# First MoE's blocks in written order on ACT, DVE, POOL and SP, and the second MoE's weight preparation in nine stages

## The chip, the cores and the metric

One core of a Trainium2 chip. TensorE (PE) multiplies, VectorE (DVE), ScalarE (ACT) and GpSimd (POOL) do the elementwise work, SyncE (SP) issues the DMA transfers. The metric is the device time of one execution in microseconds; lower is better.

## What is computed

Chunked local attention over 3072 tokens (4 x 768, 8 heads of 64), whose output runs through two feed-forward layers one behind the other.

```python
for c in range(nc):                       # chunks of 32 queries
    k_full = concat([mem_k, k[c_start-16 : c_end+8]]); v_full = ...
    a = softmax(scale * q_c @ k_full.T)
    out[c] = a @ v_full
x = out.transpose(0, 2, 1, 3).reshape(3072, 512)
h = x @ w_in                              # first MoE, 512 -> 2048 -> 512
x = relu(h) ** 2 @ w_out
g = x @ w_gate                            # second MoE, 512 -> 1536 -> 512
return (g * sigmoid(g) * (x @ w_val)) @ w_out2
```

## The kernel before

Tokens are cut into 8 blocks of 384. The first MoE's hidden dimension has 16 parts f of 128. A step is one (block t, part f): PE does the twelve hidden matmuls of the step two ahead (`hidden_pe`, L389) and then the twelve output matmuls of this one (`project_pe`, L433). Every product is three float32r passes over a high and a low half, so each operand is split into two. After the hidden matmuls ACT reads their PSUM bank (`hbank`, two of them, by parity of f) with relu (L397), squares it twice (L403 into the high half `gh`, L408), and DVE subtracts to get the low half `gl` (L414). PE's hidden matmuls two steps on write the same bank.

A step has four quarters: at each of four points between PE's half products the function `side(hs)` writes the side work of quarter `hs`. A block has 64 quarters. Side work is of two kinds:

- Attention for the next block, four units a block, 16 quarters apart. One quarter (e, the 1st, 17th, 33rd, 49th) has the value matmuls of one unit (`at_pv`, L286) and the scores of the next (`at_scores`, L164, both into `abank`); then come at e+1 the two halves of the result (x_hi on ACT L297, x_lo on DVE L301), e+2 the maximum (DVE L231, L232), e+3 and e+5 four exponentials each (ACT L240), e+7 the normalisation (DVE L253, L254, L258), e+8 and e+10 seven transposes (DVE L267), e+16 the next value matmuls. Query and key loads (`at_load`, L139) and value loads (`at_load_v`, L145) stand at e+8 for the unit due at e+16 (on SP). At the ends of a sequence DVE also sets a border of the scores (L170, L173).
- The second MoE's weights, 18 chunks of 1 MB, four to a block from block 2 on. `load2` loads a chunk (L104) 11 quarters ahead of its quarter a (4, 18, 32, 44 in a block); `prep2` at a then makes from 64-bit words float32 (`convert`: ACT scales L114, DVE shifts L115 and joins L117), four sums (POOL L478) and splits (ACT copies L481 `head`, L483 `cut`, L486 `wraw`, each with a POOL subtraction L482, L484, L487), and stores them to DRAM (`w2d`, L491, 6 to 8 transfers). Loads and block results share two `raw` buffers.

PE's instructions are in written order throughout. For the opening (a written token list) and the second MoE all engines are in written order too. In between, from step 14 of block 0 to the end of the first MoE, ACT, DVE, POOL and SP are ordered by the framework's scheduler, by its own priorities and costs: it may place an operation of `prep2` ahead of or behind relus, exponentials and loads.

In the last block's quarters the input of the second MoE is loaded, summed and split (`load_z`, `split_b1`, `sum_t`, `split_t`) and its first weights are loaded (`load_chunks`). The second MoE itself (L586, L637) is not touched.

Of the kernel before, what the change touches and what calls it, by code (L numbers as in the profile page):

```python
# [7 lines left out]
F32 = mybir.dt.float32  # L8
I32 = mybir.dt.int32
U16 = mybir.dt.uint16  # L10
R = mybir.dt.float32r
AF = mybir.ActivationFunctionType
ALU = mybir.AluOpType
# [19 lines left out]
CB = 2  # L33
# [11 lines left out]
QC = 2 * 128  # L45
# [6 lines left out]
WC = 1024  # L52
# [16 lines left out]
def attention_moe_moe_kernel(ctx, tc, att, v0, w1, w2, out):  # L69
# [9 lines left out]
    pe, act, dve, pool, sp = nc.tensor, nc.scalar, nc.vector, nc.gpsimd, nc.sync  # L79
# [4 lines left out]
    rawp = ctx.enter_context(tc.tile_pool(name="rawp", bufs=RB))  # L84
    dp = ctx.enter_context(tc.tile_pool(name="dp", bufs=1, space=DRAM))
    ps = ctx.enter_context(tc.tile_pool(name="ps", bufs=1, space=PSUM))
    w2d = dp.tile([128, NCH, 2, QC], F32, name="w2d")
# [14 lines left out]
    def load_w(src):  # L102
        t = rawp.tile([128, RAW], I32, tag="raw", name="wraw")
        sp.dma_start(out=t, in_=src.bitcast(I32))  # L104
        return t

    def convert(raw):

        words = raw.rearrange("p (n w) -> p w n", w=2)
        lower, upper = words[:, 0], words[:, 1]
        x = upper.bitcast(F32)
        act.activation(x, x, AF.Prelu, scale=2.0 ** -112, alpha=-(2.0 ** 32))  # L114
        dve.tensor_scalar(lower, lower, 29, None, ALU.logical_shift_right)  # L115
        w = rawp.tile([128, WC], F32, tag="cut", name="cut", bufs=CB)
        dve.scalar_tensor_tensor(w.bitcast(I32), upper, 3, lower, ALU.logical_shift_left, ALU.bitwise_or)  # L117
        return w


    actx = ctx.enter_context(ExitStack())
    ap = actx.enter_context(tc.tile_pool(name="ap", bufs=1))
# [202 lines left out]
    for t, n in enumerate(BLOCKS[1:], 1):  # L325
        for j in range(n):
            e = 13 * j + 12 if t == 1 else QB * (t - 1) + (j + 1) * QB // n - 15
# [12 lines left out]
    w = {}  # L340
# [76 lines left out]
    def hidden(t, f, between):  # L417
        hidden_pe(t, f, range(6))
        between()
        hidden_pe(t, f, range(6, 3 * KD))  # L420
        for fn in (relu, square, square_again, square_lo):
            fn(t, f)
# [15 lines left out]
    def project(t, f, between):  # L438
        n = nt_of[t]
        project_pe(t, f, range(6))  # L440
        between()
        project_pe(t, f, range(6, 3 * KD))
        y = [ybank[e][:, 0:n] for e in range(KD)]
        if f == NF1 - 1:
            t0 = blk0[t] * GQ
            ys = rawp.tile([128, RAW], F32, tag="raw", name="ys")[:, 0:KD * n].rearrange("p (k n) -> p k n", k=KD)
            for k in range(0, KD, 2):
                act.copy(ys[:, k], y[k])
                dve.tensor_copy(ys[:, k + 1], y[k + 1])
            sp.dma_start(out=y1d[:, :, t0:t0 + n], in_=ys)  # L450
# [6 lines left out]
    def load2(c):  # L457
        w["raw2", c] = load_w(w2[c])

    def prep2(c):  # L460
        raw = w.pop(("raw2", c))
        a = convert(raw)
        b0, b1, b2, b3 = (a[:, i * QC:(i + 1) * QC] for i in range(4))
        sums = raw.bitcast(F32)[:, 0:4 * QC]
        o0, o1, o2, o3 = (sums[:, i * QC:(i + 1) * QC] for i in range(4))
        j, kind = divmod(c, 3)
        if kind < 2:
            jobs = ((o2, b3, b2, ALU.add), (o0, o2, b0, ALU.subtract), (o1, b0, b3, ALU.subtract), (o3, b1, o0, ALU.subtract))
            first = 7 * (2 * j + kind)
            places = [w2d[:, first:first + 3:2], w2d[:, first + 5:first + 6], w2d[:, first + 1:first + 4:2], w2d[:, first + 4:first + 7:2]]  # L470
            parts = ((0, 2), (2, 4))
        else:
            jobs = ((o3, b3, b0, ALU.subtract), (o0, b2, o3, ALU.subtract), (o1, b2, b3, ALU.subtract), (o2, o0, b1, ALU.subtract))
            wo = w2d[:, GVC:].rearrange("p (i n) h c -> p i n h c", n=NP)[:, :, j]
            places = [wo[:, 0:2], wo[:, 6:7], wo[:, 2:6]]
            parts = ((0, 4),)
        for o, x, y, op in jobs:
            pool.tensor_tensor(o, x, y, op)  # L478
        head = ap.tile([128, 2 * QC], R, tag="head", name="head")
        pieces = [(a[:, 0:2 * QC], head), (b2, b3.bitcast(R))]  # L480
        act.copy(head, a[:, 0:2 * QC])  # L481
        pool.tensor_tensor(a[:, 0:2 * QC], a[:, 0:2 * QC], head.bitcast(F32), ALU.subtract)  # L482
        act.copy(b3.bitcast(R), b2)  # L483
        pool.tensor_tensor(b2, b2, b3, ALU.subtract)  # L484
        hs = raw.bitcast(R)[:, 4 * QC:8 * QC]
        act.copy(hs, sums)  # L486
        pool.tensor_tensor(sums, sums, hs.bitcast(F32), ALU.subtract)  # L487
        pieces += [(sums[:, m * QC:n * QC], hs[:, m * QC:n * QC]) for m, n in parts]
        for place, (lo, hi) in zip(places, pieces):
            for h, part in enumerate((hi.bitcast(F32), lo)):  # L490
                sp.dma_start(out=place[:, :, h], in_=part.rearrange("p (n c) -> p n c", c=QC))  # L491

    chunks = {}
    NS = NTOK // (2 * NT2)
# [60 lines left out]
    def double():  # L555
        return up.tile([128, 2 * NT2], F32, tag="tmp", name="tmp", bufs=6)
# [140 lines left out]
    def at(hs, fn, *args):  # L697
        wplan.setdefault(hs, []).append((fn, args))

    last = QB * (NB - 1)  # L700
    for c in range(NC2):
        a = QB * (P2 + c // 4) + (4, 18, 32, 44)[c % 4]
        at(a - 11, load2, c)
        at(a, prep2, c)
    for f, fn, *args in (
        (0, load_z, 0), (2, split_b1, 0, 0), (3, split_b1, 0, 1), (3, sum_t, 0, "T1"), (3, sum_t, 0, "T3"),
        (4, sum_t, 0, "T2"), (4, sum_t, 0, "T4"), (4, split_t, 0, "T2"), (5, split_t, 0, "T3"), (6, split_t, 0, "T1"),
# [5 lines left out]
    first = NF1 - lookahead  # L713
    seq = [(t, f) for t in range(NB) for f in range(NF1)]

    def side(hs):
        attention(hs)
        for fn, args in wplan.pop(hs, []):
            fn(*args)
# [5 lines left out]
        out=eye, in_=eye, pattern=[[-1, GQ]], base=0, channel_multiplier=1, compare_op=ALU.is_equal, fill=0.0,  # L725
    )
    ordered = ExitStack()
# [28 lines left out]
    for hs in range(4 * first):  # L756
        plan.pop(hs, None)
    uctx = ExitStack()
    for i, (t, f) in list(enumerate(seq))[first:]:
        if i == NF1 * (NB - 1) - 1:  # L760
            actx.close()
            up = uctx.enter_context(tc.tile_pool(name="up", bufs=1))
            late_one = up.tile([128, 1], F32, tag="one", name="one", bufs=1)
            pool.memset(late_one, 0.0)
        if i == NF1 * (NB - 1) + 8:

            act.activation(late_one, late_one, AF.Silu)
        step = iter(range(4 * i, 4 * i + 4))
        between = lambda: side(next(step))
        if i + lookahead < len(seq):  # L770
            hidden(*seq[i + lookahead], between)
        else:
            between()
        between()
        project(t, f, between)
        between()
    jobs = {}
# [24 lines left out]
            ):  # L802
                job((s, "b", at_j), fn, s + 1, *args)

    ordered.enter_context(tc.manual_schedule(engines={e.engine for e in (act, dve, pool, sp)}))
    uf += [wp.tile([128, RAW], F32, tag="w", name="uf") for _ in range(NP)]
    halves = [xp.tile([128, KD, NTM], R, tag=f"x{i}", name=f"ring{i}") for i in range(2)]
    ring += [[t[:, k] for t in halves] for k in range(KD)]
    for tags in (("gh", "gl"),) * 3 + (("r", "r"),):
        n = 3 if tags[0] == "gh" else 2  # L810
# [27 lines left out]
    for t in range(3):  # L838
        p = abanks[t][:, 0:QC]
# [6 lines left out]
        o = double()[:, 0:QC]  # L846
# [72 lines left out]
```

## Time and profile before

| | us |
|---|---|
| median of 3 runs (lowest, highest) | 1178.77 (1178.31, 1182.96) |
| profiled execution | 1179.21 |
| its span | 1177.5 |
| PE busy | 1143.6 (97%) |
| DVE, ACT, POOL busy | 725.8, 545.0, 338.8 |

In the trace the opening runs to about 109 us, blocks 1 to 7 of the first MoE to about 640 us, the second MoE to the end. Rows of the timeline give start, duration, engine, line, operation and tiles, and in brackets how long the engine stood idle before and what ended that. Rows of waits give the waiting engine and line, the releasing one, total us, number and longest. Rows by window give for each engine its busy time and instructions, then the granted clock of PE (1.00 is full), the DMA engines' share and GB/s. A PE row that is busy need not be at full pace: the granted clock says that.

### The profile page before, as it was taken

What the parts mean: (1) busy time and instruction counts of PE and PEld (TensorE: products, weight loads), DVE (VectorE), ACT (ScalarE), POOL (GpSimd) and SP (SyncE); (2) the same over time, 40 slices, a digit from 0 to 9 for tenths busy, and PEclk for the clock granted to TensorE, in tenths of its full rate; (3) what the DMA queues carried; (4) which work ended last, traced back from release to release, by engine and by line L of the source; (5) the groups of instructions that cost most, each with busy time, mean ns of one, the idle gap of its engine ahead of it and who ended that gap; (6) DMA issues with size and microseconds to landing.
All of it is one profiled execution on the core that took longest, in us unless ns stands there. A gap on an engine that the chain in (4) does not pass through costs nothing.

```text
span 1177.5 us, 22402 instructions
## 1 busy us (share of the span) xinstructions
PE 1143.6 (97%) x8804; PEld 1126.0 (96%) x8804; DVE 725.8 (62%) x1216; ACT 545.0 (46%) x1348; POOL 338.8 (29%) x317
## 2 busy tenths in 40 slices
PE   6999999899898998999999999999999999999998
PEld 6999999899898998999999999999999999999998
DVE  7996545546545555554242667956686667956654
ACT  5996555655655565654442223512252223512242
POOL 0000203515406224220000334713363333713343
PEclk9999999999899998999999999999999999999999
DMA  9733225637646556440144766787877887787772
GB/s 382 304 131 115 88 87 184 229 111 240 221 137 228 186 184 222 151 145 23 54 135 157 308 232 215 242 289 255 308 257 253 276 307 250 252 286 255 256 274 103
DMA packets 81897, 245.24 MB, mean 208 GB/s; under 512 B 6272, under 2 KB 52864, under 8 KB 61568
## 3 DMA queue, kind: packets, MB, share of 16 engines
q1 hardware_dynamic: 81792, 243.82, 60.1%
q8 instruction: 69, 1.13, 0.4%
q14 instruction: 36, 0.29, 0.1%
HBM read 198.18 MB, written 45.61 MB: 207 GB/s over the span
## 4 chain that ended last, share of the span: by engine, by line
PE 58%; DVE 2%; ACT 0%; POOL 0%; issue 0%; ACTq 0%; DVEq 0%; POOLq 0%
PE hbank L586 15%; PE yb L586 15%; PE yb L433 7%; PE hbank L389 7%; PE abank L637 7%; PE yb L637 6%; DVE ring L99 1%; PE abank L286 0%; PE hbank L651 0%; DVE zraw L544 0%; DVE z L99 0%; PE abank L164 0%; DVE w L99 0%; POOL wraw L478 0%; PE yb L651 0%
## 5 line engine op out<-in xcount | busy, mean ns | idle before, releaser
L389 PE MATMUL hbank<-x,w 128*128 128x384 f32 (+1 forms) x1548 | 297.7, 341 | 18.3 <-ACT r L397 18.3
L389 PEld LDWEIGHTS hbank<-x,w 128*128 128x128 f32 x1548 | 276.2, 193 | 20.4 <-ACT r L397 19.6
L433 PE MATMUL yb<-gh,w 128*128 128x384 f32 x1024 | 207.0, 340 | 0.0
L414 DVE TENSOR_TENSOR gl<-r,gh 128x384 fp32r<-128x384 f32 x128 | 82.0, 642 | 201.9 <-ACT r L408 200.9
L433 PEld LDWEIGHTS yb<-gh,w 128*128 128x128 f32 x1024 | 181.2, 190 | 2.2
L99 POOL TENSOR_TENSOR ring<-uf,ring 128x384 fp32r<-128x384 f32 x84 | 97.4, 1162 | 273.8 <-PE hbank L586 141.7
L573 POOL TENSOR_TENSOR uf<-uf 128x384 f32<-128x384 f32 x96 | 109.5, 1156 | 124.0 <-DVE uf L625 124.0
L586 PE MATMUL yb<-w,wst 128*128 128x384 f32 x720 | 138.3, 334 | 0.0
L586 PE MATMUL hbank<-w,wst 128*128 128x384 f32 x720 | 138.3, 334 | 0.0
L478 POOL TENSOR_TENSOR wraw<-cut 128x256 f32<-128x256 f32 x36 | 26.8, 764 | 380.5 <-DVE mx L232 305.3
L397 ACT ACTIVATE r<-hbank 128x384 f32<-128x384 f32 x128 | 63.0, 492 | 147.7 <-PE hbank L389 144.3
L586 PEld LDWEIGHTS yb<-w,wst 128*128 128x128 f32 x720 | 126.0, 188 | 0.0
L586 PEld LDWEIGHTS hbank<-w,wst 128*128 128x128 f32 x720 | 126.0, 188 | 0.0
L433 PE MATMUL yb<-gl,w 128*128 128x384 f32 x512 | 113.2, 334 | 0.0
L96 ACT CAST ring<-uf 128x384 fp32r<-128x384 f32 x168 | 85.9, 511 | 58.2 <-PE yb L637 28.9
L624 ACT ACTIVATE tmp<-tmp 128x384 f32<-128x384 f32 x48 | 25.2, 526 | 172.5 <-DVE tmp L623 172.5
L637 PE MATMUL abank<-wst,ring 128*128 128x256 f32 x756 | 93.1, 283 | 2.3 <-ACT ring L96 2.3
L637 PEld LDWEIGHTS abank<-wst,ring 128*128 128x128 f32 x756 | 91.8, 192 | 2.6 <-ACT ring L96 2.6
L433 PEld LDWEIGHTS yb<-gl,w 128*128 128x128 f32 x512 | 90.9, 188 | 0.0
L637 PE MATMUL yb<-wst,ring 128*128 128x256 f32 x702 | 86.4, 283 | 1.2 <-DVE tmp L668 1.2
L267 DVE STREAM_TRANSPOSE pT<-prob 32x256 f32<-32x256 f32 x196 | 85.2, 435 | 3.2
L637 PEld LDWEIGHTS yb<-wst,ring 128*128 128x128 f32 x702 | 85.2, 192 | 1.4 <-ACT ring L96 1.4
(128 smaller groups left out, 1499.5 us busy)
## 6 DMA issues: line engine op xcount, KB each, us to landing
wst<-w2d SPq DMA_DIRECT2D x124, 1024.0 KB, 5.0
wraw<-in_w_dram SPq DMA_DIRECT2D x34, 1024.0 KB, 7.7
qk<-in_att_dram SPq DMA_DIRECT2D x28, 464.0 KB, 4.0
w2d<-wraw SPq DMA_DIRECT2D x48, 256.0 KB, 2.5
v<-in_att_dram SPq DMA_DIRECT2D x28, 256.0 KB, 3.8
y1d<-ys SPq DMA_DIRECT2D x8, 768.0 KB, 3.8
w2d<-wraw SPq DMA_DIRECT2D x12, 512.0 KB, 4.1
zraw<-y1d SPq DMA_DIRECT2D x8, 768.0 KB, 7.9
```

The source lines that it names most:

```text
L96: act.copy(hi, src)
L99: lo_engine.tensor_tensor(lo, src, hi.bitcast(F32), ALU.subtract)
L267: dve.transpose(pT[row:row + 32, :, 32 * c:32 * c + 32], probs[u % 2][32 * c:32 * c + 32, :, col:col + 32],)
L389: pe.matmul(hbank[f % 2][:, cols], wt[:, k * 128:(k + 1) * 128], x[:, k, cols], start=i == 0, stop=i == 3 * KD - 1,)
L397: act.activation(r, hbank[f % 2][:, 0:n], AF.Relu)
L414: dve.tensor_tensor(gl, g["r"], g["gh"].bitcast(F32), ALU.subtract)
L433: pe.matmul(ybank[e][:, 0:nt_of[t]], wt[:, c:c + 128], gtile[t, f][g], start=f == 0 and p == 0, stop=f == NF1 - 1 and p == 2,)
L478: pool.tensor_tensor(o, x, y, op)
L573: pool.tensor_tensor(u_of(p, o), u_of(p, x), u_of(p, y), op)
L586: pe.matmul(to, wt[:, k * 128:k * 128 + 128], x[:, k], start=m == 0, stop=m == 5)
L624: act.activation(u4, u4, AF.Silu)
L637: pe.matmul(to[:, QC * t:QC * t + QC], u[:, rows], wt, start=p == 0 and m == 0 and t != 1, stop=p == NP - 1 and m == 2 and t != 0,)
```

## The change

`tc.manual_schedule` for ACT, DVE, POOL and SP now begins ahead of the loop over the steps from step 14 of block 0 on, and no longer only ahead of the second MoE. So all engines follow the written order from start to end. `prep2` (with `convert`) is cut into nine pieces that stand at fixed quarters after a: words at 0 (scale and shift), join at 2, sums at 3, the three splits at 4, 7 and 8 (each an ACT copy and a POOL subtraction), the three groups of stores at 9, 10 and 12. The operations of a chunk are the same.

```diff
@@ -104,20 +104,6 @@
         sp.dma_start(out=t, in_=src.bitcast(I32))
         return t
 
-    def convert(raw):
-
-
-
-        words = raw.rearrange("p (n w) -> p w n", w=2)
-        lower, upper = words[:, 0], words[:, 1]
-        x = upper.bitcast(F32)
-        act.activation(x, x, AF.Prelu, scale=2.0 ** -112, alpha=-(2.0 ** 32))
-        dve.tensor_scalar(lower, lower, 29, None, ALU.logical_shift_right)
-        w = rawp.tile([128, WC], F32, tag="cut", name="cut", bufs=CB)
-        dve.scalar_tensor_tensor(w.bitcast(I32), upper, 3, lower, ALU.logical_shift_left, ALU.bitwise_or)
-        return w
-
-
     actx = ctx.enter_context(ExitStack())
     ap = actx.enter_context(tc.tile_pool(name="ap", bufs=1))
     probs = [ap.tile([GQ, NH, GQ], F32, name=f"prob{i}") for i in range(2)]
@@ -457,38 +443,71 @@
     def load2(c):
         w["raw2", c] = load_w(w2[c])
 
-    def prep2(c):
+    prep = {}
+
+    def prep_words(c):
         raw = w.pop(("raw2", c))
-        a = convert(raw)
-        b0, b1, b2, b3 = (a[:, i * QC:(i + 1) * QC] for i in range(4))
-        sums = raw.bitcast(F32)[:, 0:4 * QC]
+        words = raw.rearrange("p (n w) -> p w n", w=2)
+        lower, upper = words[:, 0], words[:, 1]
+        x = upper.bitcast(F32)
+        act.activation(x, x, AF.Prelu, scale=2.0 ** -112, alpha=-(2.0 ** 32))
+        dve.tensor_scalar(lower, lower, 29, None, ALU.logical_shift_right)
+        prep[c] = {"raw": raw, "lower": lower, "upper": upper}
+
+    def prep_join(c):
+        q = prep[c]
+        a = q["cut"] = rawp.tile([128, WC], F32, tag="cut", name="cut", bufs=CB)
+        dve.scalar_tensor_tensor(
+            a.bitcast(I32), q["upper"], 3, q["lower"], ALU.logical_shift_left, ALU.bitwise_or
+        )
+
+    def prep_sums(c):
+        q = prep[c]
+        b0, b1, b2, b3 = (q["cut"][:, i * QC:(i + 1) * QC] for i in range(4))
+        sums = q["sums"] = q["raw"].bitcast(F32)[:, 0:4 * QC]
         o0, o1, o2, o3 = (sums[:, i * QC:(i + 1) * QC] for i in range(4))
+        if c % 3 < 2:
+            jobs = ((o2, b3, b2, ALU.add), (o0, o2, b0, ALU.subtract), (o1, b0, b3, ALU.subtract), (o3, b1, o0, ALU.subtract))
+        else:
+            jobs = ((o3, b3, b0, ALU.subtract), (o0, b2, o3, ALU.subtract), (o1, b2, b3, ALU.subtract), (o2, o0, b1, ALU.subtract))
+        for o, x, y, op in jobs:
+            pool.tensor_tensor(o, x, y, op)
+
+    def prep_split(c, part):
+        q = prep[c]
+        a = q["cut"]
+        if part == 0:
+            q["head"] = ap.tile([128, 2 * QC], R, tag="head", name="head")
+        src, hi = (
+            (a[:, 0:2 * QC], q["head"]),
+            (a[:, 2 * QC:3 * QC], a[:, 3 * QC:4 * QC].bitcast(R)),
+            (q["sums"], q["raw"].bitcast(R)[:, 4 * QC:8 * QC]),
+        )[part]
+        act.copy(hi, src)
+        pool.tensor_tensor(src, src, hi.bitcast(F32), ALU.subtract)
+        q[part] = src, hi
+
+    def prep_store(c, part):
+        q = prep[c]
         j, kind = divmod(c, 3)
         if kind < 2:
-            jobs = ((o2, b3, b2, ALU.add), (o0, o2, b0, ALU.subtract), (o1, b0, b3, ALU.subtract), (o3, b1, o0, ALU.subtract))
             first = 7 * (2 * j + kind)
-            places = [w2d[:, first:first + 3:2], w2d[:, first + 5:first + 6], w2d[:, first + 1:first + 4:2], w2d[:, first + 4:first + 7:2]]
-            parts = ((0, 2), (2, 4))
+            places = (
+                ((0, 2, w2d[:, first:first + 3:2]),), ((0, 1, w2d[:, first + 5:first + 6]),),
+                ((0, 2, w2d[:, first + 1:first + 4:2]), (2, 4, w2d[:, first + 4:first + 7:2])),
+            )
         else:
-            jobs = ((o3, b3, b0, ALU.subtract), (o0, b2, o3, ALU.subtract), (o1, b2, b3, ALU.subtract), (o2, o0, b1, ALU.subtract))
             wo = w2d[:, GVC:].rearrange("p (i n) h c -> p i n h c", n=NP)[:, :, j]
-            places = [wo[:, 0:2], wo[:, 6:7], wo[:, 2:6]]
-            parts = ((0, 4),)
-        for o, x, y, op in jobs:
-            pool.tensor_tensor(o, x, y, op)
-        head = ap.tile([128, 2 * QC], R, tag="head", name="head")
-        pieces = [(a[:, 0:2 * QC], head), (b2, b3.bitcast(R))]
-        act.copy(head, a[:, 0:2 * QC])
-        pool.tensor_tensor(a[:, 0:2 * QC], a[:, 0:2 * QC], head.bitcast(F32), ALU.subtract)
-        act.copy(b3.bitcast(R), b2)
-        pool.tensor_tensor(b2, b2, b3, ALU.subtract)
-        hs = raw.bitcast(R)[:, 4 * QC:8 * QC]
-        act.copy(hs, sums)
-        pool.tensor_tensor(sums, sums, hs.bitcast(F32), ALU.subtract)
-        pieces += [(sums[:, m * QC:n * QC], hs[:, m * QC:n * QC]) for m, n in parts]
-        for place, (lo, hi) in zip(places, pieces):
-            for h, part in enumerate((hi.bitcast(F32), lo)):
-                sp.dma_start(out=place[:, :, h], in_=part.rearrange("p (n c) -> p n c", c=QC))
+            places = (((0, 2, wo[:, 0:2]),), ((0, 1, wo[:, 6:7]),), ((0, 4, wo[:, 2:6]),))
+        lo, hi = q[part]
+        for m, n, place in places[part]:
+            for h, half in enumerate((hi.bitcast(F32), lo)):
+                sp.dma_start(out=place[:, :, h], in_=half[:, m * QC:n * QC].rearrange("p (n c) -> p n c", c=QC))
+
+    PREP = (
+        (0, prep_words), (2, prep_join), (3, prep_sums), (4, prep_split, 0), (7, prep_split, 1), (8, prep_split, 2),
+        (9, prep_store, 0), (10, prep_store, 1), (12, prep_store, 2),
+    )
 
     chunks = {}
     NS = NTOK // (2 * NT2)
@@ -701,7 +720,8 @@
     for c in range(NC2):
         a = QB * (P2 + c // 4) + (4, 18, 32, 44)[c % 4]
         at(a - 11, load2, c)
-        at(a, prep2, c)
+        for lag, fn, *args in PREP:
+            at(a + lag, fn, c, *args)
     for f, fn, *args in (
         (0, load_z, 0), (2, split_b1, 0, 0), (3, split_b1, 0, 1), (3, sum_t, 0, "T1"), (3, sum_t, 0, "T3"),
         (4, sum_t, 0, "T2"), (4, sum_t, 0, "T4"), (4, split_t, 0, "T2"), (5, split_t, 0, "T3"), (6, split_t, 0, "T1"),
@@ -756,6 +776,7 @@
     for hs in range(4 * first):
         plan.pop(hs, None)
     uctx = ExitStack()
+    ordered.enter_context(tc.manual_schedule(engines={e.engine for e in (act, dve, pool, sp)}))
     for i, (t, f) in list(enumerate(seq))[first:]:
         if i == NF1 * (NB - 1) - 1:
             actx.close()
@@ -802,7 +823,6 @@
             ):
                 job((s, "b", at_j), fn, s + 1, *args)
 
-    ordered.enter_context(tc.manual_schedule(engines={e.engine for e in (act, dve, pool, sp)}))
     uf += [wp.tile([128, RAW], F32, tag="w", name="uf") for _ in range(NP)]
     halves = [xp.tile([128, KD, NTM], R, tag=f"x{i}", name=f"ring{i}") for i in range(2)]
     ring += [[t[:, k] for t in halves] for k in range(KD)]
```

Line numbers after the change are 14 lower up to the preparation (relu is L383, the squares L389 and L394, x_hi L283, exponentials L226), and all three copies are L486.

ACT in block 2, around the third and fourth chunk prepared there, before (`head`, `cut` and `wraw` are the three copies of one chunk, L114 its scaling, `r<-hbank` is relu):

```order
L397 ACTIVATE r<-hbank_74 128x384
L403 ACTIVATE gh<-r 128x384
L408 ACTIVATE r<-r 128x384
L114 ACTIVATE wraw<-wraw 128x1024
L297 CAST x_2135<-abank 128x4x96
L481 CAST head<-cut 128x512
L483 CAST cut<-cut 128x256
L486 CAST wraw<-wraw 128x1024
L240 ACTIVATE prob_83,sm<-abank,mx 96x72 x4
L397 ACTIVATE r<-hbank_75 128x384
```

The same engine after, around the fourth chunk of block 2:

```order
L383 ACTIVATE r<-hbank_75 128x384
L389 ACTIVATE gh<-r 128x384
L394 ACTIVATE r<-r 128x384
L486 CAST head<-cut 128x512
L383 ACTIVATE r<-hbank_74 128x384
L389 ACTIVATE gh<-r 128x384
L394 ACTIVATE r<-r 128x384
L283 CAST x_2137<-abank 128x4x96
L486 CAST cut<-cut 128x256
L226 ACTIVATE prob_83,sm<-abank,mx 96x72 x4
L486 CAST wraw<-wraw 128x1024
L383 ACTIVATE r<-hbank_75 128x384
```

The three copies stood together with the scaling ahead of one relu; now one relu stands behind the first copy and one behind the other two with four exponentials.

DVE in block 2, before (L115 and L117 are shift and join of a chunk, `gl` is the subtraction, `pT` the transposes that the value matmuls read):

```order
L117 SCALAR_TENSOR_TENSOR cut<-wraw 128x1024
L414 TENSOR_TENSOR gl<-r,gh 128x384 x2
L115 TENSOR_SCALAR wraw<-wraw 128x1024
L117 SCALAR_TENSOR_TENSOR cut<-wraw 128x1024
L301 TENSOR_TENSOR x_2980<-abank,x_2979 128x4x96
L231 TENSOR_REDUCE mx<-abank 96x8
L232 TENSOR_SCALAR mx<-mx 96x8
L414 TENSOR_TENSOR gl<-r,gh 128x384
L253 TENSOR_SCALAR sm<-sm 96x8
L254 RECIPROCAL sm<-sm 96x8
L258 TENSOR_TENSOR prob_83<-prob_83,sm 96x8x72
L267 STREAM_TRANSPOSE pT<-prob_83 32x8x32 x3
```

After, from the third chunk's join to the transposes of that unit (gl is L400, x_lo L287, join L460, maximum L217, normalisation L239 to L244):

```order
L460 SCALAR_TENSOR_TENSOR cut<-wraw 128x1024
L217 TENSOR_REDUCE mx<-abank 96x8
L218 TENSOR_SCALAR mx<-mx 96x8
L400 TENSOR_TENSOR gl<-r,gh 128x384
L239 TENSOR_SCALAR sm<-sm 96x8
L240 RECIPROCAL sm<-sm 96x8
L244 TENSOR_TENSOR prob_84<-prob_84,sm 96x8x72
L400 TENSOR_TENSOR gl<-r,gh 128x384
L253 STREAM_TRANSPOSE pT<-prob_84 32x8x32 x7
```

One join stands between two units' worth of attention, where two stood close together; the seven transposes now stand together.

SP in block 2, before (`w2d` is a chunk's stores, `qk` and `v` attention's loads):

```order
L491 DMA w2d<-cut 128x256
L139 DMA qk<-in_att_dram 128x928
L491 DMA w2d<-cut 128x256
L491 DMA w2d<-wraw 128x2x256 x4
L145 DMA v<-in_att_dram 128x512
L491 DMA w2d<-head 128x2x256
L491 DMA w2d<-cut 128x2x256
```

After, from the fourth chunk's stores to the block's result:

```order
L505 DMA w2d<-head 128x2x256
L505 DMA w2d<-cut 128x2x256
L505 DMA w2d<-cut 128x256 x2
L505 DMA w2d<-wraw 128x2x256 x4
L131 DMA v<-in_att_dram 128x512
L125 DMA qk<-in_att_dram 128x928
L104 DMA wraw<-in_w_dram 128x2048
L436 DMA y1d<-ys 512x1x384
```

The loads of v and qk, before among and behind some stores, stand behind all stores of the fourth chunk.

## Rows read from the trace of the kernel before

**Rows 1.** The page: PE, busy us, share of the span, instructions

```profile
PE 1143.6 (97%) x8804; PEld 1126.0 (96%) x8804; DVE 725.8 (62%) x1216; ACT 545.0 (46%) x1348; POOL 338.8 (29%) x317
```

**Rows 2.** PE's waits, longest first in total

```profile
PE hbank L389 <- ACT r L397: 18.3, 4, 4.6
```

**Rows 3.** Windows: blocks 1 to 5 of the first MoE

```profile
109.42:182.78 73.36, 73.36 (x641) 71.52 (x641) 36.17 (x73) 38.99 (x124) 7.39 (x7) 1.00 0.28 92
182.78:262.57 79.79, 75.20 (x642) 73.05 (x641) 44.38 (x81) 47.12 (x136) 29.38 (x28) 0.98 0.58 193
262.57:343.59 81.02, 76.44 (x642) 74.28 (x641) 43.77 (x79) 46.98 (x136) 29.35 (x28) 0.96 0.58 190
343.59:423.36 79.77, 75.19 (x641) 73.04 (x641) 44.39 (x81) 47.20 (x136) 29.33 (x28) 0.98 0.58 193
423.36:504.24 80.88, 76.28 (x641) 74.13 (x641) 43.78 (x79) 47.07 (x136) 29.36 (x28) 0.96 0.58 190
```

**Rows 4.** Timeline of PE, block 2: hidden matmuls

```profile
206.98 2.24 PE L389 MATMUL hbank<-x,w 128*128 128x384 f32 x12
...
220.06 3.73 PE L389 MATMUL hbank<-x,w 128*128 128x384 f32 x12 [4.59 <-ACT r L397]
```

**Rows 5.** Timeline of ACT, the same stretch

```profile
210.08 1.13 ACT L114 ACTIVATE wraw<-wraw 128x1024 f32<-128x1024 f32 x1
...
214.43 0.62 ACT L481 CAST head<-cut 128x512 fp32r<-128x512 f32 x1 [2.86 <-issue]
215.89 0.41 ACT L483 CAST cut<-cut 128x256 fp32r<-128x256 f32 x1 [0.84 <-POOL wraw L478]
217.37 1.04 ACT L486 CAST wraw<-wraw 128x1024 fp32r<-128x1024 f32 x1 [1.08 <-POOL wraw L478]
...
219.51 0.49 ACT L397 ACTIVATE r<-hbank 128x384 f32<-128x384 f32 x1
```

**Rows 6.** Timeline of DVE, the same stretch

```profile
210.21 2.22 DVE L414 TENSOR_TENSOR gl<-r,gh 128x384 fp32r<-128x384 f32 x1 [4.03 <-ACT r L408]
...
213.13 1.23 DVE L117 SCALAR_TENSOR_TENSOR cut<-wraw 128x1024 int32<-128x1024 int32 x1
```

**Rows 7.** Timeline of POOL, the same stretch

```profile
209.61 2.40 POOL L487 TENSOR_TENSOR wraw<-wraw 128x1024 f32<-128x1024 f32 x1
```

**Rows 8.** Timeline of PE in block 1, a step with attention

```profile
146.10 2.25 PE L389 MATMUL hbank<-x,w 128*128 128x384 f32 x12
148.28 0.88 PE L286 MATMUL abank<-pT,v 128*64 128x96 f32 x16
...
151.96 2.24 PE L389 MATMUL hbank<-x,w 128*128 128x384 f32 x12
```

**Rows 9.** Timeline of ACT, the same step

```profile
148.38 0.49 ACT L397 ACTIVATE r<-hbank 128x384 f32<-128x384 f32 x1 [2.56 <-PE hbank L389]
...
149.46 0.52 ACT L408 ACTIVATE r<-r 128x384 f32<-128x384 f32 x1
```

**Rows 10.** Timeline of DVE, the same unit

```profile
150.02 0.56 DVE L414 TENSOR_TENSOR gl<-r,gh 128x384 fp32r<-128x384 f32 x1 [3.60 <-ACT r L408]
...
150.96 0.75 DVE L231 TENSOR_REDUCE mx<-abank 96x8 f32<-96x576 f32 x1
...
156.61 2.68 DVE L267 STREAM_TRANSPOSE pT<-prob 32x256 f32<-32x256 f32 x6
```

**Rows 11.** Groups by line: busy us, mean ns, idle before

```profile
L478 POOL TENSOR_TENSOR wraw<-cut 128x256 f32<-128x256 f32 x36 | 26.8, 764 | 380.5 <-DVE mx L232 305.3 <-DVE cut L117 75.2
```

**Rows 12.** Line 258, the normalisation: ns min/median/max

```profile
L258 DVE TENSOR_TENSOR prob<-prob,sm x28: 753/754/2912, 38.7 to 550.9; 96x576 f32<-96x576 f32 x28
```

**Rows 13.** Line 145, value loads, window 182 to 562

```profile
DMA to landing us min/median/max: 2.6/3.8/5.7
```

**Rows 14.** Line 491, stores, window 182 to 562: ns min/median/max

```profile
L491 SPq DMA_DIRECT2D w2d<-wraw x56: 359/433/924, 196.0 to 519.6; - x56
```

**Rows 15.** Timeline of DVE in block 7

```profile
588.99 1.95 DVE L544 TENSOR_TENSOR zraw<-zraw 128x768 f32<-128x768 f32 x2 [3.41 <-DMA zraw<-y1d]
```

## The prediction

> **What bounds the kernel now.** I read the page's busy shares first: TensorE (PE) is busy for 97% of the span [rows 1]. So time can only come out of PE's idle time or out of its slow stretches, and the next view is the list of PE's own waits. Its largest entry is one kind of wait, four times, 4.6 us each: a hidden-layer matmul (L389) that needs a PSUM bank which ACT's relu (L397) has not emptied yet [rows 2].
>
> The table by block of the first MoE says what they cost. Block 1 takes 73.36 us and PE is busy for all of it. Blocks 2 to 5 take 79.79, 81.02, 79.77 and 80.88 us, at a granted clock of 0.98 or 0.96 instead of 1.00 [rows 3]. Their excess is 321.46 - 4 x 73.36 = **28.0 us**. 18.3 us of it are the waits themselves [rows 2]; the other 9.7 us are matmuls at the lower of TensorE's two clock levels (1.2 instead of 2.4 GHz) just behind a wait: the twelve matmuls at 220.06 take 3.73 us, those at 206.98 take 2.24 [rows 4].
>
> Why relu comes late is read from ACT at the same place [rows 5]. The hidden matmuls that start at 206.98 [rows 4] could be read 2.28 us later (in an undisturbed block they start at 146.10 and relu at 148.38 [rows 8, 9]), that is at 209.26. Their relu starts at 219.51, 10.25 us late. In between ACT does the weights of one chunk in one go: the scaling, then three copies that wait 2.86, 0.84 and 1.08 us, then four exponentials. The first copy waits for DVE's join at 213.13, which stood behind a subtraction that took 2.22 us instead of 0.56 [rows 6, 10] while POOL's 2.40 us operation ran [rows 7]; the other two wait for POOL. Relu stands behind all that in ACT's order.
>
> **The limit, from the undisturbed rhythm.** Call T the start of a step's hidden matmuls. Relu can start at T+2.28, the second square is over at T+3.88 [rows 8, 9], DVE's subtraction at T+4.48 [rows 10], attention's value matmuls start at T+2.18 [rows 8]. A step with attention takes 5.86 us (146.10 to 151.96 [rows 8]), one without 4.16 (4 x 5.86 + 12 x 4.16 = 73.36). The bank is wanted again two steps on, so relu (0.49) may start 8.32 - 2.28 - 0.49 = about **5.5 us late** before PE waits. The attention of the next unit is due 18.34 us (5.86 + 3 x 4.16) on, at 20.5 after T.
>
> **The change part by part.** No instruction is added or removed: 18 chunks with the same operations, and PE's order stays. What moves is where they stand.
>
> *Copies on ACT.* They stand at steps +4, +7 and +8 after the chunk's first quarter, with relus between. The place to test is the tightest, chunks 3 and 4 of a block.
> Chunk 3, from T of step 8: subtraction over at 4.48, half-result x_lo to 4.9 (in rows 10 the maximum starts 0.94 after the subtraction did), join 1.23 [rows 6] to 6.15, maximum 0.75 [rows 10] and its scaling to 7.1, four exponentials 1.2 (the end of the third copy to relu's start in rows 5 is 1.1) to 8.4, head copy 0.62 [rows 5] to 9.0. Relu of step 9 was possible at 5.86 + 2.28 = 8.14: 0.9 late. Relu and squares 1.6, four exponentials, the two other copies 0.41 and 1.04 [rows 5] to 13.25; POOL's four sums (0.76 each [rows 11], 6.2 to 9.2) are done by then, so nothing waits. Relu of step 10 was possible at 12.30: 0.95 late.
> Chunk 4, from T of step 12: the join follows the transposes of chunk 3's unit and ends at 3.6, head copy to 4.2, relu 1.9 late; sums to 6.6, second copy to 7.0, exponentials to 9.6, third copy to 10.65, relu of step 13 (possible at 8.14) **2.5 late**. In blocks 2 and 4 a boundary memset on DVE stands ahead of x_hi in both places; it shifts these by 0.76 and 1.0, to at most 4.0 late. All are inside 5.5. So the four waits go, and nothing is late in their place on PE: **-28.0 us**, the clock's part included, since block 1 without a wait has clock 1.00 [rows 3].
>
> *Transposes on DVE.* The value matmuls have no second buffer, so here DVE's lateness is PE's at once. After chunk 3: exponentials end at 11.8, normalisation to 13.6 (held by one short POOL operation), subtraction at 14.85 held until POOL's 2.40 us operation ends at 16.0, over at 16.45, seven transposes (2.68 for six [rows 10], so 3.1) to 19.5; due at 20.5. Slack 1.0, and 0.25 in blocks 2 and 4. After chunk 4: 18.75, in blocks 2 and 4 20.1. Cost between 0 and what a whole held normalisation adds, 2.91 - 0.75 = 2.16 us [rows 12], less the slack: at most 1.9 at four places in blocks 2 and 4 and 1.2 at the two chunk-3 places of blocks 3 and 5, 10 us together. I take 0, because the lock is already in the sum once at each place.
> No row shows a transpose beside a POOL operation. The Trainium skill ("SBUF — State Buffer", Who interferes with whom) says that a DVE instruction with one SBUF input, outside its two-port modes, does not contend with GpSimd, while one with two SBUF inputs waits for GpSimd's whole instruction; by that rule the transposes keep their length and the 0 stands; were they held like the normalisation, the sum would be up to 10 us higher.
>
> *SP's queue.* Value and query loads (L145, L139) now stand behind all stores of chunk 4, where before they stood among or ahead of stores. Those stores wait for POOL's last operation, over at 13.2 from T of step 12; three stores follow at 0.43 us of issue each [rows 14], so the value load goes out near 14.6 and lands 3.8 us later by the median, 5.7 at worst [rows 13]: 18.4 to 20.3, due 20.5. Blocks 2 and 4 are 0.7 later, so 0.5 late at worst, twice. I take 0, and keep 1 us for the range.
>
> *Chunks in other blocks.* Before, chunk 1 was prepared in block 1 and one chunk in block 6; now none and two. Both blocks ran without a wait beside a chunk, chunks 1 and 2 stand 14 quarters apart, and my sum for them gives relu 0.7 late and transposes 2.4 early. Cost 0; without that cover it would be a wait like those of [rows 2], 7.0 us with its clock.
>
> *Last block.* The second MoE's input (sums and splits on DVE and ACT) now stands at fixed quarters. Steps 3 and 4 ask DVE for three operations of 0.97 us each [rows 15] beside the subtraction's 0.56, 3.5 us in a step of 4.16, and ACT's copy behind the second sum ends before the next relu is due. Cost 0, up to 1.
>
> **Sum.** Profiled execution 1179.2 (span 1177.5), less 28.0, is 1151.2; median of the runs 1178.77 less 28.0 is **1150.8 us**.
>
> **Rivals.**
> *A. A remainder.* DVE's transposes or the value loads come late at the tight places. For it: slacks of 0.25 to 1.0 against a lock of up to 2.16. Against: the lock is already counted, and the transposes come behind POOL's last operation. Price 3 to 10 us: 1154 to 1161.
> *B. In-order waiting at each chunk (slower).* ACT no longer passes a copy whose input is late, so one late join or sum holds relu at every one of 18 chunks, not at four. It decides from a relu 5.5 late; I get 4.0. Each us beyond costs 18; from 28.0/18 = 1.6 beyond it is slower than before, and with a full wait and its clock (28.0/4 = 7.0) each, 1150.8 + 126 = 1277. For it: the three copies did wait 4.8 us in a row before [rows 5]. Against: those waits came from the three copies standing together; now 1 to 3 quarters lie between.
> *C. No change.* The late join comes from the POOL lock, not from ACT's order, and the lock stays: four waits remain, 1178. Against: the join was only 2.9 of the 10.25 us.
>
> **How the numbers follow.** Forecast (1149 to 1153) 0.76, A 0.15, C 0.04, B 0.05. The range must leave out no more than 0.2: it takes in A up to its upper price, 1149 to 1161. A kernel this long can be told from no change at about 0.5%, 5.9 us; the forecast and A are both beyond: faster 0.91, same 0.04, slower 0.05.
>
> **What would show it.** Right: PE's list has no wait on ACT's relu, blocks 2 to 5 take 73.4 us each at clock 1.00, ACT's copies of one chunk have a relu between them. A shows as PE waiting at L286's new line for DVE or a load. B shows as many waits of PE on relu, with ACT waiting for DVE's join or POOL's sums. Wrong would be four waits of 4.6 us elsewhere in the blocks, or a PE wait in the last block or at the start of the second MoE, which I take as untouched.

## The result and the profile after

The median of the changed kernel is 1153.18 us (four runs, 1150.67 to 1155.30) against 1179.99 for the kernel before, run beside it: ratio 0.9769, interval 0.974 to 0.9799. The forecast was 1150.8 in a range of 1149 to 1161, faster: right in sign and, to 0.2%, in size.

The page of the changed kernel, PE with busy us, share of the span and instructions (before: [rows 1]):

```profile
PE 1137.2 (99%) x8804; PEld 1120.9 (97%) x8804; DVE 719.7 (62%) x1216; ACT 551.7 (48%) x1348; POOL 348.1 (30%) x317
```

PE's waits in the changed kernel, the first two by their totals (before: [rows 2]):

```profile
PE yb L150 <- DMA qk<-in_att_dram: 4.3, 1, 4.3
PE abank L656 <- ACT ring L96: 2.3, 2, 1.2
```

No wait on relu is left: of the list's nine entries L150, L192 and L210 wait in the opening and L656 in the second MoE, and none is in the blocks between. Blocks 1 to 5 of the changed kernel, windows (columns as in [rows 3]: PE, PEld, DVE, ACT, POOL, then clock, DMA share, GB/s):

```profile
113.51:186.87 73.36, 73.36 (x641) 71.52 (x641) 32.76 (x74) 36.96 (x120) 0.00 (x0) 1.00 0.20 67
186.87:260.23 73.36, 73.36 (x641) 71.52 (x641) 42.66 (x78) 48.05 (x135) 31.27 (x28) 1.00 0.54 188
260.23:333.59 73.36, 73.36 (x641) 71.52 (x641) 44.52 (x82) 48.31 (x136) 31.24 (x28) 1.00 0.62 216
333.59:406.95 73.36, 73.36 (x641) 71.52 (x641) 42.24 (x78) 48.24 (x136) 31.27 (x28) 1.00 0.60 207
406.95:480.31 73.36, 73.36 (x641) 71.52 (x641) 44.57 (x82) 48.02 (x136) 31.25 (x28) 1.00 0.62 214
```

Each of the four blocks that took 79.77 to 81.02 us now takes 73.36, with PE busy throughout and the granted clock at 1.00: 28.0 us gone, as the sum had it. What comes behind is as long as before: from 480.31 to the end 673.29 us, from 504.24 before [rows 3] 673.26.

The profiled execution took 1155.3 us (span 1153.6), only 23.9 below that of before. The other 4.1 us lie ahead of block 1, which starts at 113.51 and not at 109.42 [rows 3]. Most of it is one row in the opening, here in the timeline of PE of the changed kernel:

```profile
31.85 10.46 PE L375 MATMUL hbank<-x,w 128*128 128x288 f32 x40
```

and here the same forty matmuls in the kernel before:

```profile
31.07 7.14 PE L389 MATMUL hbank<-x,w 128*128 128x288 f32 x40
```

Neither has a wait ahead of it. This is not the change: the row takes 6.98, 7.11, 9.32, 6.99 and 9.08 us in the experiments E1 to E5 below and 10.56 in E6, and E4 (6.99) and E6 have the order of the changed kernel here. How long it takes depends on when the clock rises in it (last section). It moves profiled executions by up to 3.6 us against each other, and the forecast did not know of it. Behind the opening, from the start of block 1 to the end, the profiled executions take 1068.1 us before and 1040.1 after, 28.0 apart. E4's opening ends 4.4 us earlier than this one (109.11 against 113.51); with it the execution of 1155.3 would be one of 1150.9, an estimate, and the forecast was 1150.8.

The place that the prediction worked through, the fourth chunk of block 2, in the changed kernel. ACT:

```profile
245.79 0.62 ACT L486 CAST head<-cut 128x512 fp32r<-128x512 f32 x1 [4.16 <-DVE cut L460]
246.31 0.49 ACT L383 ACTIVATE r<-hbank 128x384 f32<-128x384 f32 x1
...
249.16 0.41 ACT L486 CAST cut<-cut 128x256 fp32r<-128x256 f32 x1
...
252.42 1.05 ACT L486 CAST wraw<-wraw 128x1024 fp32r<-128x1024 f32 x1
253.36 0.50 ACT L383 ACTIVATE r<-hbank 128x384 f32<-128x384 f32 x1
```

PE at the same place:

```profile
247.76 2.24 PE L375 MATMUL hbank<-x,w 128*128 128x384 f32 x12
...
256.08 2.24 PE L375 MATMUL hbank<-x,w 128*128 128x384 f32 x12
```

Where three copies waited in a row [rows 5], only the first still waits, 4.16 us, and for most of that no relu could start (the first moment was 241.90 + 2.28 = 244.18). A relu stands behind it, at 246.31 and 2.13 us late, and one behind the other two. That last one could start at 247.76 + 2.28 = 250.04 and starts at 253.36: 3.32 us late, the most in blocks 2 to 5. The bank is wanted at 256.08, and PE does not wait.

### The profile page after: what moved, and what is told of

Same layout as the page of the kernel before. It is cut to its first block, busy times and chain, and to the rows that moved or that the text cites. A ratio compares the mean times of both kernels' runs of the same rounds, so it can differ in the third digit from the quotient of the medians.

```text
span 1153.6 us, 22369 instructions
## 1 busy us (share of the span) xinstructions
PE 1137.2 (99%) x8804; PEld 1120.9 (97%) x8804; DVE 719.7 (62%) x1216; ACT 551.7 (48%) x1348; POOL 348.1 (30%) x317
## 3 DMA queue, kind: packets, MB, share of 16 engines
q8 instruction: 69, 1.13, 0.4%
## 4 chain that ended last, share of the span: by engine, by line
PE 96%; DVE 2%; DMA 1%; ACT 0%; issue 0%; SPq 0%; ACTq 0%; DVEq 0%
PE hbank L375 24%; PE yb L419 24%; PE hbank L605 15%; PE yb L605 15%; PE abank L656 7%; PE yb L656 6%; PE abank L272 2%; PE abank L150 2%; DVE ring L99 1%; PE hbank L210 1%; DMA first_v<-in_v_dram 1%; PE hbank L670 0%; DVE zraw L563 0%; DVE z L99 0%; DVE w L99 0%
## 5 line engine op out<-in xcount | busy, mean ns | idle before, releaser
L375 PE MATMUL hbank<-x,w 128*128 128x384 f32 (+1 forms) x1548 | 293.9, 338 | 0.0
L400 DVE TENSOR_TENSOR gl<-r,gh 128x384 fp32r<-128x384 f32 x128 | 87.2, 682 | 228.7 <-ACT r L394 228.5
L419 PEld LDWEIGHTS yb<-gh,w 128*128 128x128 f32 x1024 | 178.7, 188 | 2.2
L383 ACT ACTIVATE r<-hbank 128x384 f32<-128x384 f32 x128 | 63.0, 492 | 133.5 <-PE hbank L375 133.1
L656 PE MATMUL abank<-wst,ring 128*128 128x256 f32 x756 | 93.1, 283 | 2.3 <-ACT ring L96 2.3
L656 PEld LDWEIGHTS abank<-wst,ring 128*128 128x128 f32 x756 | 91.8, 192 | 2.6 <-ACT ring L96 2.6
L656 PE MATMUL yb<-wst,ring 128*128 128x256 f32 x702 | 86.4, 283 | 1.2 <-DVE tmp L687 1.2
L226 ACT ACTIVATE prob<-abank,mx 96x72 f32<-96x72 f32 x224 | 67.6, 310 | 40.6 <-DVE mx L218 40.3
```

The lines of the kernel that those rows point to most:

```text
L226: act.activation(probs[u % 2][:, h, 0:WK], s["s"][:, r, i], AF.Exp, bias=s["mx"][:, r, i:i + 1], scale=SCALE, accum_out=s["sm"][:, h],)
L375: pe.matmul(hbank[f % 2][:, cols], wt[:, k * 128:(k + 1) * 128], x[:, k, cols], start=i == 0, stop=i == 3 * KD - 1,)
L383: act.activation(r, hbank[f % 2][:, 0:n], AF.Relu)
L400: dve.tensor_tensor(gl, g["r"], g["gh"].bitcast(F32), ALU.subtract)
L419: pe.matmul(ybank[e][:, 0:nt_of[t]], wt[:, c:c + 128], gtile[t, f][g], start=f == 0 and p == 0, stop=f == NF1 - 1 and p == 2,)
L656: pe.matmul(to[:, QC * t:QC * t + QC], u[:, rows], wt, start=p == 0 and m == 0 and t != 1, stop=p == NP - 1 and m == 2 and t != 0,)
```

## The experiments

Three questions: whether the stages or the written order brings the gain; what the stages' lags are for; and whether "5.5 us late" is the limit. Whether POOL's lock of DVE (a DVE operation that stands still while one of POOL's runs, rival C) has a part was a fourth, but no run varies the lock. The theory is the prediction's: relu late behind the three copies. The rivals are B (a written order makes ACT wait at every chunk) and C.

### E1: the stages without the order

Preparation in nine stages, but ACT, DVE, POOL and SP are still ordered by the scheduler up to the second MoE.

```diff
-    ordered.enter_context(tc.manual_schedule(engines={e.engine for e in (act, dve, pool, sp)}))
     for i, (t, f) in list(enumerate(seq))[first:]:
...
+    ordered.enter_context(tc.manual_schedule(engines={e.engine for e in (act, dve, pool, sp)}))
     uf += [wp.tile([128, RAW], F32, tag="w", name="uf") for _ in range(NP)]
```

> The nine stages at their quarters, but ACT, DVE, POOL and SP ordered by the scheduler again up to the second MoE. My theory: the scheduler pulls the three copies of a chunk together ahead of one relu whatever the quarters are (on ACT the fourth chunk of block 2 stands again as scaling, head, cut, wraw, four exponentials, relu), so all four PE waits of 4.6 us and the 28 us of blocks 2 to 5 are back: about 1180 us, ratio to the kernel before 0.997 to 1.003. Rival (the stages alone do it): no PE wait on relu, about 1153 us.

Measured: 1180.37 us, ratio to before 0.9998, interval 0.9987 to 1.001. PE's waits, their first row:

```profile
PE hbank L375 <- ACT r L383: 18.4, 4, 4.6
```

and ACT in block 2 of E1:

```profile
214.14 0.62 ACT L486 CAST head<-cut 128x512 fp32r<-128x512 f32 x1 [2.86 <-issue]
...
219.22 0.49 ACT L383 ACTIVATE r<-hbank 128x384 f32<-128x384 f32 x1
```

This is [rows 2] again, and the head copy's wait of 2.86 us, with relu at 219.22, is [rows 5] again: the scheduler put the pieces back together, and relu stood behind them as before. The quarters at which the stages are written do nothing by themselves.

### E2: the order without the stages

Written order as in the changed kernel, but all nine pieces of a chunk at its first quarter, as the old function had them.

```diff
     PREP = (
-        (0, prep_words), (2, prep_join), (3, prep_sums), (4, prep_split, 0), (7, prep_split, 1), (8, prep_split, 2),
-        (9, prep_store, 0), (10, prep_store, 1), (12, prep_store, 2),
+        (0, prep_words), (0, prep_join), (0, prep_sums), (0, prep_split, 0), (0, prep_split, 1), (0, prep_split, 2),
+        (0, prep_store, 0), (0, prep_store, 1), (0, prep_store, 2),
     )
```

> Written order on all engines, but all nine stages at the chunk's first quarter, so that ACT meets scaling and all three copies in one go. My theory: the order alone does not do it. By the same sums as in the prediction relu is 5.8 us late behind the first chunk of a block, 4.2 and 4.3 behind the second and third, about 9 behind the fourth (its join waits for the transposes): one PE wait of about 3.5 us a block and one of 0.3, with the lower clock behind the long one: 4 x (3.8 + 2) = 23 us, about 1176 us (1165 to 1182). Rival (written order alone is enough): about 1153 us, no PE wait on relu. Rival (in-order waiting at every chunk): 18 waits, over 1200 us.

Measured: 1210.88 us, ratio 1.0276 (1.0246 to 1.0307): 31 us slower than before, beyond the 1165 to 1182 of the expectation. By its time the run fits the rival of a wait at every chunk (over 1200), but not by its waits, since PE waits for relu 7 times and not 18. PE's waits:

```profile
PE abank L272 <- DMA v<-in_att_dram: 22.0, 7, 4.4
PE hbank L375 <- ACT r L383: 13.2, 7, 2.7
...
PE abank L272 <- DVE pT L253: 3.6, 4, 0.9
```

The relus wait 13.2 us, but the largest term is one that the expectation had not: value matmuls that wait for their values. SP's queue in E2 says why (issue time, duration, source and destination):

```profile
192.71 0.39 SPq L505 DMA_DIRECT2D w2d<-head  x1
196.52 1.37 SPq L505 DMA_DIRECT2D w2d<-cut  x3
198.02 3.24 SPq L505 DMA_DIRECT2D w2d<-wraw  x4
201.32 0.48 SPq L104 DMA_DIRECT2D wraw<-in_w_dram  x1
201.86 0.45 SPq L131 DMA_DIRECT2D v<-in_att_dram  x1
```

and PE:

```profile
207.50 1.55 PE L272 MATMUL abank<-pT,v 128*64 128x96 f32 x16 [4.30 <-DMA v<-in_att_dram]
```

The loads are written behind eight stores, and SP stands at each store until its data exist (for the head copies alone 164.5 us in 18 waits in this run). So the value load goes out at 201.86 and not before; its landing takes 5.8 us by the median of its line in E2, and PE wants it at 203.20. With 0.5 us on a shift (L454) the four kinds make 39.3 us. The stretches at the lower clock are 37.5 us together and cost about half, 18.8: 58.1 over the changed kernel, measured 1210.88 - 1153.18 = 57.7.

### E3: only the three copies together again

```diff
-        (0, prep_words), (2, prep_join), (3, prep_sums), (4, prep_split, 0), (7, prep_split, 1), (8, prep_split, 2),
+        (0, prep_words), (2, prep_join), (3, prep_sums), (4, prep_split, 0), (4, prep_split, 1), (4, prep_split, 2),
```

> As the changed kernel, but the three copies all at the chunk's fourth quarter instead of 4, 7 and 8. My theory: relu of the step of the fourth chunk's head copy becomes 5.8 us late in blocks 3 and 5 and 7.3 in blocks 2 and 4 against a limit of 5.5: PE waits of 0.3 and 1.8 us there, and as much again at the value matmuls, whose transposes had 1.1 us left in blocks 2 and 4: 4 to 8 us in all, 1157 to 1161 us, clock 1.00. Rival (the spread of the copies is not needed once join and sums stand ahead): 1153 us and no wait. Rival (the copies standing together is the whole cause): four waits of 4.6 us, about 1180 us.

Measured: 1176.04 us, ratio 0.9975 (0.9964 to 0.9986). All but 4 us of the gain is lost, and not where it was expected. PE's waits in E3:

```profile
PE abank L272 <- DVE pT L253: 11.6, 5, 2.4
...
PE hbank L375 <- ACT x L283: 3.9, 2, 2.0
```

None is for relu, though relus are up to 6.63 us late. A chain through DVE takes its place. ACT, DVE and PE in E3:

```profile
199.81 1.05 ACT L486 CAST wraw<-wraw 128x1024 fp32r<-128x1024 f32 x1 [0.29 <-POOL wraw L474]
200.76 0.48 ACT L383 ACTIVATE r<-hbank 128x384 f32<-128x384 f32 x1
...
202.40 2.22 DVE L400 TENSOR_TENSOR gl<-r,gh 128x384 fp32r<-128x384 f32 x1 [4.61 <-ACT r L394]
204.54 3.12 DVE L253 STREAM_TRANSPOSE pT<-prob 32x256 f32<-32x256 f32 x7
...
207.72 1.30 PE L272 MATMUL abank<-pT,v 128*64 128x96 f32 x16 [2.39 <-DVE pT L253]
```

A late relu makes a late subtraction (2.22 us, beside POOL's 2.40 us operation, as in [rows 6, 7]); the transposes stand behind it on DVE, and the value matmuls have no second buffer. Twice (255.81 and 413.12) hidden matmuls wait for x_hi (L283): the first hidden matmuls of the next block, written at step 14, need the last unit's result. The prediction did not list that dependency. The five waits for transposes are at the units behind a block's first chunk, where the changed kernel has 2.7 to 2.8 us of slack, and not where the expectation looked, behind the fourth. So the copies standing together do not by themselves make the waits of [rows 2]: with join and sums ahead of them relu keeps inside its limit, and it takes all the operations of a chunk at one quarter (E2, E5) to bring waits on relu back. Waits of 15.5 us and half of 13.6 us at the lower clock make 22.3; measured 1176.04 - 1153.18 = 22.9.

### E4: relu held back by a known amount

The changed kernel, with activations on a spare tile ahead of a relu at three places without preparation: 21 and 29 in block 1, 41 in block 6.

```diff
+    slow = ap.tile([128, 128], F32, name="slow")
+    pool.memset(slow, 0.0)
+    LADDER = {QB + 28: 21, QB + 44: 29, QB * 6 + 56: 41}
...
     def side(hs):
         attention(hs)
+        for _ in range(LADDER.get(hs, 0)):
+            act.activation(slow, slow, AF.Relu)
```

> The changed kernel with extra work on ACT (128x128 in-place relus on an own tile, about 0.3 us each) just ahead of one relu: 21 in block 1 at quarter 28, 29 in block 1 at quarter 44, 41 in block 6 at quarter 56. ACT is free for 2.56 us ahead of a relu there, so relu comes about 4.0, 6.4 and 10 us late. My theory (a relu may start 5.5 us late before PE waits): no wait, a wait of about 0.9 us, a wait of about 4.6 us; the lower clock shows behind the last alone and costs about 2 us. Rival (PE is sensitive to relu at once): waits of 4, 6 and 10 us. Total 6 to 9 us over the changed kernel.

Measured: 1158.45 us in one run, 5.3 over the changed kernel's median and about 7.5 over the 1150.9 us worked out above for this opening (expected: 6 to 9). Relus are 4.40, 7.13 and 11.23 us late, and only the third makes PE wait; a wait of 0.9 us was expected at the second. Second place, PE and ACT in E4:

```profile
159.97 2.24 PE L375 MATMUL hbank<-x,w 128*128 128x384 f32 x12
...
169.39 0.47 ACT L383 ACTIVATE r<-hbank 128x384 f32<-128x384 f32 x1
...
170.00 2.29 PE L375 MATMUL hbank<-x,w 128*128 128x384 f32 x12
```

Third place:

```profile
540.34 2.24 PE L375 MATMUL hbank<-x,w 128*128 128x384 f32 x12
...
539.97 13.97 ACT L743 ACTIVATE slow<-slow 128x128 f32<-128x128 f32 x41
553.85 0.47 ACT L383 ACTIVATE r<-hbank 128x384 f32<-128x384 f32 x1
...
554.37 4.02 PE L375 MATMUL hbank<-x,w 128*128 128x384 f32 x12 [5.55 <-ACT r L383]
```

At the third, 11.23 late less 5.55 of waiting leaves 5.68: the limit of 5.5 is right within 0.2, where two steps without attention follow each other (before: 10.25 late, 4.59 waited, 5.66). At the second, 159.97 to 170.00 is an attention step and a plain one, 5.86 + 4.16 = 10.02, so the limit there is 10.02 - 2.28 - 0.49 = 7.25; 7.13 late just fits. The first place has the same two steps, so its 4.40 tests little. That is also why E3's relus, next to an attention step, made no wait.

### E5: as E2, but the stores at their late quarters

Loads no longer stand behind unready stores; all else of a chunk is at its first quarter. The diff is against E2.

```diff
-        (0, prep_store, 0), (0, prep_store, 1), (0, prep_store, 2),
+        (9, prep_store, 0), (10, prep_store, 1), (12, prep_store, 2),
```

> Like the run with written order alone (all operations of a chunk at its first quarter, 1210.9 us), but the chunk's stores at quarters 9, 10 and 12 as in the changed kernel. My theory for the 22.0 us in which the value matmuls waited for value loads there: SP stood at stores whose data POOL had not made, with the loads behind them; now the loads stand ahead of the stores, so these 22 us and their share of the lower clock go, and the waits for relu (13.2) and for transposes (3.6) stay: 1153.2 + 17 + 5 to 9 for the clock = 1175 to 1180 us. Rival (the loads were slow, not late): 1205 us or more, with the value matmuls still waiting for loads.

Measured: 1187.47 us, ratio 1.006 (1.0042 to 1.0078), 23.4 us less than E2. PE's waits in E5:

```profile
PE hbank L375 <- ACT r L383: 15.0, 8, 2.7
PE abank L272 <- DVE pT L253: 10.5, 9, 1.4
```

The 22.0 us on the loads are gone: the stores ahead of them were their cause. The transposes' wait grew from 3.6 to 10.5 us, since PE used to arrive at those places after a wait for values and now arrives before DVE. The relus' grew by 1.8 us. These two make most of what E5 lies above its expectation. ACT at the fourth chunk of block 2 in E5, and PE behind it:

```profile
248.06 0.62 ACT L486 CAST head<-cut 128x512 fp32r<-128x512 f32 x1 [4.72 <-issue]
250.34 0.41 ACT L486 CAST cut<-cut 128x256 fp32r<-128x256 f32 x1 [1.66 <-POOL wraw L474]
...
251.97 0.48 ACT L383 ACTIVATE r<-hbank 128x384 f32<-128x384 f32 x1
...
252.51 3.67 PE L375 MATMUL hbank<-x,w 128*128 128x384 f32 x12 [2.66 <-ACT r L383]
```

The written order holds ACT for 4.72 and 1.66 us at copies whose inputs are not there, with relu behind them: rival B as it was described, 2.7 us at most instead of a full wait of 4.6. Waits (25.5) and half of 13.6 us at the lower clock (6.8) make 32.3; measured 1187.47 - 1153.18 = 34.3. The 2.0 us between them are not accounted for.

### E6: the changed kernel again, unaltered

> The changed kernel again, to tell 28.0 us (my sum) from 26.8 (the first four runs): 1150.8 to 1153.2 us. In the profile blocks 2 to 5 take 73.36 us each; what differs from run to run is the opening.

Measured: 1153.16 us (five runs, 1150.56 to 1154.36) against 1180.34, ratio 0.9762, interval 0.9744 to 0.9779. The forecast's 28.0 of 1178.77 is the ratio 0.9762.

## Why the prediction was right, point by point

- **What bounds the kernel.** Right. PE's four waits on relu and the low-clock matmuls behind them were all of blocks 2 to 5's excess; with the waits gone the blocks take block 1's 73.36 us.
- **The limit.** 5.5 for steps without attention (measured 5.66 and 5.68), but the text gave it for all places. Next to an attention step it comes to 7.25: E4's 7.13 and E3's 6.63 made no wait there, and no relu was later.
- **Copies on ACT.** Right that a relu now stands between them. Lateness in the changed kernel, us:

| place | predicted, blocks 3 and 5 | measured | predicted, blocks 2 and 4 | measured |
|---|---|---|---|---|
| chunk 3, two relus | 0.9, 0.95 | 0.58, 0.36 | at most 4.0 in all | 1.40, 1.18 |
| chunk 4, first two relus | 1.9, 2.5 | 1.29, 1.78 | at most 4.0 in all | 2.13, 3.32 |

- **Transposes on DVE.** Cost 0 was right, and this was the tight place: the smallest slack of the value matmuls is 0.69 us behind chunk 3 in blocks 2 and 4 (predicted 0.25) and 1.53 in blocks 3 and 5 (1.0); behind chunk 4 it is 1.13 and 2.67 (0.4 and 1.75). POOL's lock fell on the subtraction ahead of or behind them, not on the normalisation in full (1.26 us at most, near chunk 3). Here DVE and PE behind chunk 3 of block 2 of the changed kernel:

```profile
238.69 1.65 DVE L400 TENSOR_TENSOR gl<-r,gh 128x384 fp32r<-128x384 f32 x1 [1.05 <-ACT r L394]
240.26 3.12 DVE L253 STREAM_TRANSPOSE pT<-prob 32x256 f32<-32x256 f32 x7
...
244.07 0.88 PE L272 MATMUL abank<-pT,v 128*64 128x96 f32 x16
```

  and DVE and POOL behind chunk 2:

```profile
219.63 3.12 DVE L253 STREAM_TRANSPOSE pT<-prob 32x256 f32<-32x256 f32 x7
...
220.45 2.39 POOL L487 TENSOR_TENSOR wraw<-wraw 128x1024 f32<-128x1024 f32 x1
```

  The subtraction at 238.69 takes 1.65 us, beside a POOL operation that runs from 237.23 for 2.69 us. The transposes at 219.63 run beside nearly all of POOL's 2.39 us and take 3.12, as the seven do beside no POOL operation (258.17 to 261.29). So the row that was missing before now exists. It agrees with the Trainium skill ("SBUF — State Buffer", Who interferes with whom), by which an instruction with one SBUF input outside the two-port modes is not held.
- **SP's queue.** The value load of block 2's end went out 15.55 us after T of step 12 (241.90 to 257.45; predicted 15.3) and landed 3.56 later, 1.4 us ahead of its matmuls. Cost 0 was right. The worst case was mis-sized: value loads of blocks 2 to 5 land after 3.4/5.1/7.1 us (lowest, median, highest) instead of the 2.6/3.8/5.7 of [rows 13] (that they now go out among other loads is a likely reason, not shown); 7.1 at that place would have been a wait of about 2 us. E2 shows the price when the queue's order is wrong: 22.0 us.
- **Chunks in other blocks, last block.** Cost 0, as predicted: 673.29 against 673.26 us behind block 5.
- **Rival B.** Wrong for this change, and right in part for its neighbours: E2 and E5, which differ from it in the lags alone, are slower than before, with 7 and 8 waits on relu and not 18. What decided is the lags, but not only those that the prediction set against it, one to three quarters between the copies: without these E3 still has no wait on relu, so the join and sums ahead of the copies count too. "Slower from 1.6 us beyond the limit" was too simple, though: E3 loses 22.9 us with no relu beyond its limit, through the transposes. A condition on relu alone does not bound the loss.
- **Rival C.** Wrong. The lock stayed (the subtraction's mean is 682 ns, before 642; POOL is busy 348.1 us, before 338.8), and the waits went. In [rows 6, 10] it costs the subtraction 2.22 - 0.56 = 1.66 us; taken out of the 10.25 us, that would leave 8.6, still beyond 5.66: an estimate. A kernel of before without the lock was not run.

What the sum left out is the opening: the median lies 2.4 us above the forecast, and the two profiled executions of the changed kernel, 1155.3 and 1154.36 us, both have a long row of forty matmuls there. That the executions of 1150.6 us have a short one is likely but not shown, since none of them was profiled.

## What to carry to other kernels

Writing an in-order engine's order out by hand brings little (E3, 4 us), or costs (E2, E5), unless each piece stands where its input is ready: the same operations made 1210.9, 1187.5, 1176.0 or 1153.2 us, by the lags alone. When work is spaced, go by the consumer with the least buffering (here the value matmuls, 0.7 us of slack, not the double-buffered bank with 5.5), and follow a late operation through the next engine's queue as well (E3). Stores whose data are not ready hold the loads written behind them in the same queue (22.0 us of waits in E2, none in E5).

## What the runs showed of the hardware that was not expected

**The clock behind a short wait is not a fixed price.** In E3 PE waits five times for transposes, for 2.30 to 2.39 us, at the same instruction. Windows behind two of them (granted clock is the third column from the right):

```profile
290.00:294.00 4.00, 4.00 (x33) 3.83 (x23) 3.00 (x5) 2.57 (x9) 0.00 (x0) 0.58 0.97 340
...
366.50:371.00 4.50, 4.50 (x81) 4.29 (x82) 3.37 (x7) 1.90 (x5) 0.00 (x0) 1.00 0.84 303
```

The first, behind a wait of 2.30 us, is at 1.2 GHz for most of the stretch; the second, behind another wait of 2.30 us, stays at 2.4. Of fifteen waits of 1.95 to 2.66 us in E2, E3 and E5, ten came with a stretch at 1.2 GHz; of those of 3.6 us and more in all runs, every one; of those of up to 1.5 us, none (all counted from block 1 on). In E3 four of the seven waits of this kind had such a stretch, which together cost about 6.8 us, half the time they lasted. Why the same wait goes one way or the other stays open.

**A clock column of 1.00 can mean that nothing was recorded.** The forty matmuls of the opening take 6.98 to 7.14 us in four profiled executions and 9.08 to 10.56 in four, with PE busy throughout and the clock column at 1.00 in both. The first clock record of each trace starts only within this row, and the column prints 1.00 ahead of it too. That record, the rise to 2.4 GHz, starts at 32.37 to 32.91 us in the four short executions (E4, E1, E2, before) and at 36.94, 37.36, 40.04 and 40.85 us in the four long ones (E5, E3, E6, the changed kernel). Here are 3.5 us of PE in E4, the same 3.5 us in E6, and 3.5 us in block 3 of the kernel before at a recorded 0.50 (PE alone, matmuls of 384 columns in all three, their number in brackets):

```profile
36.00:39.50 3.50, 3.50 (x22) 1.00 1.03 425
...
36.00:39.50 3.50, 3.50 (x13) 1.00 1.04 425
...
300.50:304.00 3.50, 3.50 (x13) 0.50 1.02 335
```

E6 has ahead of its first record the pace of 1.2 GHz, and E4 behind its own has the pace of 2.4. So the clock makes the difference, and how many matmuls a stretch holds tells it where the column does not. E4 and E6 have the same instructions on PE up to 32.3 us, with starts within 0.01 us of each other; why the clock then rises 7.7 us later in one of them stays open.
